# Where the maxima of staged weights stand among the steps of a two-branch attention kernel

## The chip, the core and the metric

The kernel runs on one core of one Trainium2 chip. The metric is the device time of one execution in microseconds (us). TensorE (PE), VectorE (DVE), ScalarE (ACT), GpSimd (POOL) and the queue of SyncE (SP), which issues most transfers, each work through their own list of instructions in order, and wait for one another by semaphores.

## What is computed

Two attention blocks over the same input, with 32 heads of 20 features each, mixed by a gate of one number per row:

```python
B, S, D = 1, 2048, 640; H = 32
qkv = (x @ wqkv).reshape(B, S, 3, H, 20)
p = softmax(einsum("bhqd,bhkd->bhqk", q, k) * 20 ** -0.5)
attend = einsum("bhqk,bhkd->bhqd", p, v).reshape(B, S, D) @ wo
g = sigmoid((A_x * gate_w).sum(-1, keepdims=True))
out = g * attend(A_x, A_wqkv, A_wo) + (1 - g) * attend(A_x, B_wqkv, B_wo)
```

## The kernel before

**Units and steps.** The 2 x 32 heads are cut into 16 groups of four heads (`g`, 0 to 15). For each group the 2048 queries are cut into four blocks of 512 (`qb`), and for each block the keys are worked through in eight steps (`NS`). That makes 512 steps, counted by `G`; group `g` begins at step `b = 32 g`. A step holds two **half-steps**. In each, PE makes four products of scores (L684, into a bank of PSUM), ACT takes their exponentials (L687, `pt`), and PE multiplies those by the values into the accumulator `acc` (L702, eight instructions). Beside that, PE makes scores of later units a first time (L626) so that DVE can take their row maxima (L637, or L630 on ACT with L634 on DVE), 15 steps ahead. There are seven banks that the products share; which one is taken is decided while the program is written, by a model of when each comes free (`take`, `give`, `spend`).

**Projections between.** A half-step may also hold a block of products of a projection (L419): queries and keys of a coming group (128, 168 or 176 columns wide), values (160), or outputs (up to 320). Weights are split in two 16-bit halves for this, after scaling by a power of two, so the largest absolute value of each weight matrix is needed first.

**The chain of a scale.** A piece of weights of 128 x 5 x 160 numbers is loaded into `wstage` (two buffers) by SP. DVE takes its largest absolute value (`largest`, L270). For the queries and keys, and for the output weights, `max_tasks` writes this in two pieces, rows 0:3 and rows 3:5 of the five, two turns apart. For the values, `weights_v` writes it in one. The maximum then goes through memory to all partitions: store (L212), ten turns, load into `srows` (L216), 18 turns, and then DVE's small instructions (L220 and `powers`), which give the factor (`r_v`, `r_qk`, `r_o`) that POOL splits the weights by. `scales_o` also makes the factors `f_o` of the output rows, by two DVE instructions on 128 x 16 numbers (L263, L265).

**What sets the order.** Nothing is scheduled by the chip. The step loop calls `scores` eight times in a step, in an order written out in `STEP`; after each, `advance()` lets every running side chain (`side`) go on to its next `yield`. One such turn is an eighth of a step. After the fourth, the tasks entered for that step by `at(G, ...)` are written. So `QKMAX`, `OMAX` and the numbers in the calls of `at` decide beside which step an instruction stands in each engine's list. `QKMAX` entries are loads and maxima in turn, two steps each; those of `OMAX` are load, factor (POOL, L280), maximum, one step each.

**Steps in which sums are turned.** After the second values of a step with `G % 8 == 0`, a block of queries is done. `take_acc` has DVE transpose `acc` into `ot` (L789), take a reciprocal (L794), and, six turns later, POOL scale it (L797); 16 turns after that, DVE transposes it again (L800). The next values (L702), half a step after the block's last, write `acc` anew and so have to wait for the first transpose. About one and a half steps after it stand the reduction and small transpose that end a block's maxima (L644, L647).

```python
if G % NS == 0 and k == 2 and G < STEPS:
    side.append(take_acc(*unit_of(G - 1)[:2]))
    advance()
```

Of the kernel before, what the change touches and what calls it, by code (L numbers as in the profile page):

```python
# [11 lines left out]
F32 = mybir.dt.float32  # L12
# [7 lines left out]
P = 128  # L20
# [22 lines left out]
OWAIT = 24  # L43
PACE = 2
AFROM, ADUE, ADUES = -24, -8, 4
QKMAX = (0, 10, 42, 10)
VEARLY = 338
OMAX, OSPLIT = (134, 346), (151, 362)
OUTS = ((166, 5.2), (257, 5.8), (398, 4.5), (466, 2.5))
OWAITS = (40, 20, 20, 10)  # L50
OFINE = (16, 16, 6, 16)
# [20 lines left out]
def kernel(  # L72
# [183 lines left out]
    def scales_v(gg, maxima):  # L256
        return scales_by_dram(maxima, 1, lambda r, inv: set_v(gg, r, inv))

    def scales_o(z, maxima):
        def then(r, inv):  # L260
            nc.vector.tensor_copy(r_o[z], r)
            yield
            nc.vector.tensor_scalar(f_o[z], gates[:, z, :], inv, inv_x, op0=OP.mult, op1=OP.mult)  # L263
            yield
            nc.vector.tensor_scalar(f_o[z], f_o[z], 1.0 / QKS, None, op0=OP.mult)  # L265

        return scales_by_dram(maxima, 1, then)

# [13 lines left out]
    def max_tasks(srcs, finish, by=None):  # L282


        m = wts.tile([P, 2, 8], F32, name="wmax", tag="wmax", bufs=2)
        tasks = []
        for k, parts in enumerate(srcs):
            for i, (src, c0) in enumerate(parts):
                st = {}

                def load(st=st, src=src, c0=c0):
                    st["t"] = weight_chunk(src, c0, 160)

                def factor(st=st):
                    by_rows(st["t"], by)

                def reduce(st=st, k=k, i=i):
                    largest(m[:, k, 2 * i:2 * i + 1], st["t"][:, 0:3])

                    def other():  # L300
                        yield
                        yield
                        largest(m[:, k, 2 * i + 1:2 * i + 2], st["t"][:, 3:NC])

                    side.append(other())

                tasks += [load, reduce] if by is None else [load, factor, reduce]

        def last():
            m2 = wts.tile([P, 2], F32, name="m2", tag="m2", bufs=2)  # L310
            n = len(srcs)
            nc.vector.tensor_reduce(m2[:, :n], m[:, :n, :2 * len(srcs[0])], axis=AX.X, op=OP.max)
            side.append(finish(m2))

        return tasks + [last]
# [236 lines left out]
    def weights_v(gg):  # L552

        z, i = divmod(gg, NG // 2)
        st = {}

        def load():
            st["t"] = weight_chunk(wqkv[z], 2 * D + i * 160, 160)

        def scale():  # L560
            m = wts.tile([P, 1], F32, name="m1", tag="m1", bufs=2)
            largest(m, st["t"])
            return scales_v(gg, m)

        def split():
            hi, lo = v_tiles(gg)
            split_weights(st["t"], r_v[gg], hi[:, :, :160], lo[:, :, :160])

        return load, scale, split
# [19 lines left out]
    def sigmoids():  # L589

        g, h = gates[:, 0, :], gates[:, 1, :]
        nc.vector.tensor_scalar(h, g, 1.0, None, op0=OP.add)
        nc.vector.reciprocal(g, h)
        nc.vector.tensor_scalar(h, g, -1.0, 1.0, op0=OP.mult, op1=OP.add)


# [483 lines left out]
        for k, f in enumerate(fs):  # L1080
            at(G + k * gap, f)

    at(4, sigmoids)
    step = NQ * NS
    for g in range(2 * NG):
        b = g * step
        n = g + 1
        if n < 2 * NG:
            parts = APARTS.get(n, 3)
            fill += [((-8, 15)[g] if g < 2 else b + AFROM, b + ADUE + ADUES * ch if g else 4 + 3 * ch, parts, project_a(n, ch))  # L1090
                     for ch in range(4)]
            if n + 1 < 2 * NG:
                tasks(b + 2 if g else 9, 3, weights_a(n + 1))
            i = g // 4 + 1
            if i < 4:
                if g % 4 == 0:
                    z, c0 = i // 2, 320 * (i % 2)
                    srcs = max_tasks([[(wqkv[z], part * D + c0 + 160 * k) for k in range(2)] for part in range(2)],
                                     lambda m, i=i: scales_qk(i, m))
                    tasks(b + QKMAX[i], 2, srcs)  # L1100
                if g % 4 == 2:
                    tasks(b + 6, 3, weights_r(i))
                    parts = RPARTS.get(i, 3)
                    fill += [(b + 12, b + 26 + 6 * ch if i == 1 else b + 22 + 4 * ch, parts, project_r(i, ch)) for ch in range(4)]
            gg = g // 2 + 1
            if gg < NG and g % 2 == 0:
                load, scale, split = weights_v(gg)
                at(max(b - 11, 0), load)
                if gg < NG - 1:
                    at(max(b - 8, 3), lambda scale=scale: side.append(scale()))  # L1110
                at(max(b - 1, 10), split)
                fill += [(max(b + 2, 12), b + 2 * step - 4 + j // 2, 2, project_v(gg, j)) for j in range(0, NT, 2)]
    early = weights_v(NG - 1)
# [165 lines left out]
```

## Time and profile before

| what | value |
|---|---|
| time, median of 3 runs (lowest to highest) | 2754.22 us (2753.87 to 2754.22) |
| the profiled execution's own time, its span | 2753.79 us, 2752.0 us |
| PE, DVE, ACT, POOL busy, share of the span | 99%, 89%, 92%, 24% |
| the chain that ended last | PE 93%, DVE 3%, ACT 1% |
| granted TensorE clock, mean | 0.997 |

A matmul's end is modelled in the profile, so a PE that stands still for a few tenths of a microsecond still shows as busy. A better measure of a half-step is the time from the start of one group of values (L702) to the start of the next.

### The profile page before, as it was taken

Reading aid. Unit: us, or ns where it says so; the run is one execution under the profiler, and the core shown is the slowest. Engines: PE = TensorE matmul, PEld = TensorE weight load, DVE = VectorE, ACT = ScalarE, POOL = GpSimd, SP = SyncE. Lnnn points to the kernel's source line nnn. Section 1 sums busy time; section 2 is a strip of 40 time slices with the busy share of each in tenths; the row PEclk is TensorE's granted clock in tenths of the full one; section 3 lists DMA queues with packets and bytes.
Section 4 is the critical chain, followed back from the end, with each engine's and each line's share of the span. In section 5 each row is a group of like instructions: output and inputs, shape, how many; then the busy total and the mean of one; then the engine's idle time right before and its main releaser. Section 6 shows DMA issues by size and latency. Waiting matters only on the chain.

```text
span 2752.0 us, 62213 instructions
## 1 busy us (share of the span) xinstructions
PE 2718.3 (99%) x23277; PEld 938.3 (34%) x23277; DVE 2441.0 (89%) x4785; ACT 2527.8 (92%) x5128; POOL 667.6 (24%) x909
## 2 busy tenths in 40 slices
PE   7999999999999999999999999999999999999999
PEld 3433333333333332333333333333333333333222
DVE  7789899999999989888888998989988898999992
ACT  4999999999999999999999999999999999999997
POOL 6232122222123421312221121222342202210111
PEclk8999999999999999999999999999999999999999
DMA  4021102010120211102012231221201112122112
GB/s 142 17 57 26 31 15 44 7 30 17 25 55 18 63 41 49 43 9 61 20 41 67 61 81 29 55 57 51 66 16 42 27 53 64 32 77 61 49 48 77
DMA packets 177008, 125.58 MB, mean 46 GB/s; under 512 B 105280, under 2 KB 147064, under 8 KB 176704
## 3 DMA queue, kind: packets, MB, share of 16 engines
q1 hardware_dynamic: 174160, 120.31, 17.2%
q8 instruction: 182, 2.98, 0.5%
q0 software_dynamic: 1600, 0.96, 0.2%
q14 instruction: 122, 1.00, 0.1%
q10 hardware_dynamic: 944, 0.33, 0.0%
HBM read 55.53 MB, written 31.86 MB: 32 GB/s over the span
## 4 chain that ended last, share of the span: by engine, by line
PE 93%; DVE 3%; ACT 1%; DMA 1%; POOL 1%; issue 0%; SPq 0%; POOLq 0%; ACTq 0%; DVEq 0%
PE acc L702 35%; PE bank L626 20%; PE bank L419 20%; PE bank L684 18%; DVE mpart L637 1%; ACT pt L687 1%; DMA ws<-in_A_wqkv_dram 0%; PE bank L878 0%; DVE rl L634 0%; DVE ot L789 0%; DMA kt<-mrow 0%; DMA xs<-in_A_x_dram 0%; DVE m L270 0%; ACT rl L630 0%; SPq L465 0%
## 5 line engine op out<-in xcount | busy, mean ns | idle before, releaser
L687 ACT ACTIVATE pt<-bank 128x512 f32<-128x512 f32 x4096 | 2166.3, 613 | 140.2 <-PE bank L684 97.5
L637 DVE TENSOR_REDUCE mpart<-bank 128x1 f32<-128x512 f32 x2944 | 1845.0, 681 | 219.4 <-PE bank L626 118.3
L702 PE MATMUL acc<-pt,v 128*21 128x512 f32 x8192 | 1081.7, 600 | 0.6 <-DVE ot L789 0.5
L684 PE MATMUL bank<-qt,kt 64*128 64x512 f16 x4096 | 1036.7, 380 | 1.7 <-DVE mpart L637 0.6
L626 PE MATMUL bank<-kt,qt 60*128 60x512 f16 x3520 | 1006.5, 380 | 4.5 <-ACT pt L687 2.2
L626 PEld LDWEIGHTS <-qt 60*128 60x128 f16 x4096 | 239.2, 94 | 900.6 <-issue 832.8
L634 DVE CUSTOM_DVE_ANT_0 rl<-bank,rl 128x512 f32<-128x512 f32 x576 | 386.5, 677 | 6.7 <-ACT rl L630 2.5
L630 ACT ACTIVATE rl<-bank 128x512 f32<-128x512 f32 x576 | 338.2, 597 | 7.3 <-PE bank L626 6.9
L684 PEld LDWEIGHTS <-kt 64*128 64x128 f16 x4096 | 230.2, 94 | 175.9 <-issue 65.4
L702 PEld LDWEIGHTS acc<-pt,v 128*21 128x21 f32 x8192 | 143.0, 99 | 428.7 <-issue 423.5
L419 PE MATMUL bank<-xx,wbh 128*128 128x168 f16 (+3 forms) x2480 | 287.7, 236 | 1.4 <-DVE wbh L958 1.0
L419 PE MATMUL bank<-xx,wbl 128*128 128x168 f16 (+3 forms) x1240 | 257.5, 235 | 0.0
L797 POOL TENSOR_TENSOR ot<-ot,sq 128x512 f32<-128x512 f32 x63 | 66.1, 1049 | 774.9 <-DVE sq L794 756.4
L419 PEld LDWEIGHTS <-wbh 128*128 128x128 f16 x2480 | 192.8, 98 | 111.1 <-issue 104.7
L626 PE MATMUL bank<-kd,qt 60*128 60x512 f16 x576 | 203.5, 379 | 0.7
L419 PE MATMUL bank<-woh,o_in 128*128 128x320 f16 (+3 forms) x700 | 157.7, 290 | 0.6 <-ACT pt L687 0.6
L419 PE MATMUL bank<-wvh,xx 128*128 128x160 f16 (+1 forms) x1280 | 156.7, 234 | 0.6 <-DVE mpart L634 0.6
L448 POOL CAST cq<-fs 128x512 f16<-128x512 f32 x60 | 36.7, 612 | 487.0 <-ACT fs L446 470.4
L419 PEld LDWEIGHTS <-xx 128*128 128x128 f16 x1920 | 131.1, 97 | 59.4 <-issue 56.5
L419 PE MATMUL bank<-wvl,xx 128*128 128x160 f16 (+1 forms) x640 | 137.7, 232 | 0.0
L419 PEld LDWEIGHTS <-wbl 128*128 128x128 f16 x1240 | 121.2, 98 | 4.3 <-issue 0.9
L419 PEld LDWEIGHTS <-o_in 128*128 128x128 f16 (+1 forms) x1050 | 87.4, 97 | 91.5 <-issue 68.2
(147 smaller groups left out, 1246.4 us busy)
## 6 DMA issues: line engine op xcount, KB each, us to landing
y_scr<-y_out SPq DMA_DIRECT2D x48, 320.0 KB
y_out<-y_scr SPq DMA_DIRECT2D x32, 320.0 KB
kt<-cq SPq DMA_DIRECT2D x120, 80.0 KB
o_scr<-on SPq DMA_DIRECT2D x240, 40.0 KB
o_in<-o_scr SPq DMA_DIRECT2D x64, 96.0 KB
kt<-cq SPq DMA_DIRECT2D x136, 40.0 KB
wstage<-in_B_wqkv_dram SPq DMA_DIRECT2D x13, 400.0 KB
xs<-in_A_x_dram SPq DMA_DIRECT2D x8, 640.0 KB
```

Source lines behind the costliest of these rows:

```text
L419: nc.tensor.matmul(out_ap, a, b, start=(k == 0), stop=(k == len(pairs) - 1))
L448: nc.gpsimd.tensor_copy(hi, f)
L626: nc.tensor.matmul(pt, QT[g % 2][r, pair, q0:q0 + P], k, start=True, stop=True)
L630: nc.scalar.activation(relus[u, j], pt, AF.Relu)
L634: nc.vector.tensor_tensor_reduce(rl, pt, rl, 1.0, LOW, OP.add, OP.max, m)
L637: nc.vector.tensor_reduce(m, pt, axis=AX.X, op=OP.max)
L684: nc.tensor.matmul(et, KT[g % 2][r, pair, kt * P:(kt + 1) * P], QT[g % 2][r, pair, qb * QB:(qb + 1) * QB], start=True, stop=True)
L687: nc.scalar.activation(pt, et, AF.Exp, scale=factor(g // 4))
L702: nc.tensor.matmul(acc[32 * h:32 * h + VW, :], V[(g // 2) % 2][:, kt, (g % 2) * GH + h, :], ptiles.pop((G, kk, h)), start=(kt == 0), stop= ...
L797: nc.gpsimd.tensor_tensor(t3, t3, sq.unsqueeze(2).to_broadcast([P, 16, 32]), op=OP.mult)
```

## The change

The first half of each staged maximum and its second half now stand six turns apart instead of two (`max_tasks`), and the values' maximum, which was one instruction, is made the same way with one small instruction that joins the halves. The steps at which they begin are moved: `QKMAX` from 10, 42, 10 to 11, 40, 11, `OMAX[0]` from 134 to 132, and the values' load and maximum one step later. `f_o` is made by one DVE instruction on one number per partition, and one POOL instruction on 128 x 16. The three small instructions that turn the gate's exponentials into the two gates are set two turns apart.

```diff
-QKMAX = (0, 10, 42, 10)
+QKMAX = (0, 11, 40, 11)
-OMAX, OSPLIT = (134, 346), (151, 362)
+OMAX, OSPLIT = (132, 346), (151, 362)
...
-            nc.vector.tensor_scalar(f_o[z], gates[:, z, :], inv, inv_x, op0=OP.mult, op1=OP.mult)
+            f = wts.tile([P, 1], F32, name="fo", tag="fo", bufs=1)
+            nc.vector.tensor_scalar(f, inv, inv_x, 1.0 / QKS, op0=OP.mult, op1=OP.mult)
             yield
-            nc.vector.tensor_scalar(f_o[z], f_o[z], 1.0 / QKS, None, op0=OP.mult)
+            nc.gpsimd.tensor_scalar(f_o[z], gates[:, z, :], f, None, op0=OP.mult)
...
                     def other():
-                        yield
-                        yield
+                        yield from turns(6)
                         largest(m[:, k, 2 * i + 1:2 * i + 2], st["t"][:, 3:NC])
...
         def scale():
-            m = wts.tile([P, 1], F32, name="m1", tag="m1", bufs=2)
-            largest(m, st["t"])
-            return scales_v(gg, m)
+            m = wts.tile([P, 3], F32, name="m1", tag="m1", bufs=2)
+            largest(m[:, 0:1], st["t"][:, 0:3])
+            yield from turns(6)
+            largest(m[:, 1:2], st["t"][:, 3:NC])
+            yield
+            nc.vector.tensor_reduce(m[:, 2:3], m[:, 0:2], axis=AX.X, op=OP.max)
+            yield from scales_v(gg, m[:, 2:3])
...
         nc.vector.tensor_scalar(h, g, 1.0, None, op0=OP.add)
+        yield from turns(2)
         nc.vector.reciprocal(g, h)
+        yield from turns(2)
         nc.vector.tensor_scalar(h, g, -1.0, 1.0, op0=OP.mult, op1=OP.add)
...
-    at(4, sigmoids)
+    at(4, lambda: side.append(sigmoids()))
...
-                at(max(b - 11, 0), load)
+                at(max(b - 10, 0), load)
                 if gg < NG - 1:
-                    at(max(b - 8, 3), lambda scale=scale: side.append(scale()))
+                    at(max(b - 7, 3), lambda scale=scale: side.append(scale()))
```

The lists of PE and ACT keep every instruction in its place; only the banks that they name differ from step 3 on. On DVE, one place is step 56, the turn of sums before the third group's values are needed. The list of before has there (`m` is the values' maximum, `rl,mpart` and `mpart` are row maxima of scores, `ot` and `sq` belong to the turn, `mneg` and `mt` to the end of a block's maxima):

```order
L270 TENSOR_REDUCE m_5311<-wstage 128x1
L634 ISA rl,mpart<-bank_94,rl 128x512
L634 ISA mpart 128x1
L789 STREAM_TRANSPOSE ot<-acc 128x512
L794 RECIPROCAL sq<-ot 128x16
L637 TENSOR_REDUCE mpart<-bank_91 128x1
```

The changed list, from behind the turn on, has:

```order
L271 TENSOR_REDUCE m_5388<-wstage 128x1
L643 TENSOR_REDUCE mpart<-bank_93 128x1
L643 TENSOR_REDUCE mpart<-bank_91 128x1
L650 TENSOR_REDUCE mneg_75<-mpart 128x16
L653 STREAM_TRANSPOSE mt<-mneg_75 128x32
L643 TENSOR_REDUCE mpart<-bank_90 128x1
L643 TENSOR_REDUCE mpart<-bank_89 128x1
L643 TENSOR_REDUCE mpart<-bank_91 128x1
L643 TENSOR_REDUCE mpart<-bank_92 128x1
L271 TENSOR_REDUCE m_5388<-wstage 128x1
L566 TENSOR_REDUCE m_5388<-m_5388 128x1
```

The maximum has gone from ahead of the transpose to one and two steps behind it, on either side of `mneg` and `mt`. The other place on DVE is the output factor of the first branch, in step 150 before (`es` is the maximum spread over the partitions and its powers, `r_o` and `f_o` what comes of it):

```order
L174 TENSOR_SCALAR es<-es 128x1
L261 COPY r_o_117<-es 128x1
L637 TENSOR_REDUCE mpart<-bank_91 128x1
L263 TENSOR_SCALAR f_o_119<-gates,es,inv_x 128x16
L637 TENSOR_REDUCE mpart<-bank_95 128x1
L265 TENSOR_SCALAR f_o_119<-f_o_119 128x16
```

After the change, about two steps sooner, DVE has:

```order
L174 TENSOR_SCALAR es<-es 128x1
L643 TENSOR_REDUCE mpart<-bank_92 128x1
L261 COPY r_o_117<-es 128x1
L264 TENSOR_SCALAR fo<-es,inv_x 128x1
L643 TENSOR_REDUCE mpart<-bank_94 128x1
```

and the product with the gates stands in POOL's list, behind the split of a turned block (`on`) and ahead of a projection's (`cq`):

```order
L809 CAST on<-ob 128x512
L810 TENSOR_TENSOR on<-ob,on 128x512
L266 TENSOR_SCALAR f_o_119<-gates,fo 128x16
L448 CAST cq<-fs 128x512
```

Two wide DVE instructions have become one narrow one, and POOL has one more.

## The prediction

> **What bounds the kernel now.** I read the page first, then the waits of PE, then the lengths of single half-steps.
>
> ```profile
> span 2752.0 us, 62213 instructions
> PE 2718.3 (99%) x23277; PEld 938.3 (34%) x23277; DVE 2441.0 (89%) x4785; ACT 2527.8 (92%) x5128; POOL 667.6 (24%) x909
> ```
>
> PE is the bound, and the change takes no work from it. So the only time to be won is time in which PE stands still for another engine. The waits of PE seem to leave almost none:
>
> ```profile
> PE bank L183 <- DVE wm L924: 11.0, 1, 11.0
> ...
> PE bank L626 <- ACT pt L687: 2.2, 8, 0.5
> ...
> PE bank L419 <- ACT pt L687: 0.6, 1, 0.6
> ```
>
> (engine, line, what it waited for: us in total, times, longest.) The largest is in the start, which the change leaves alone. But a modelled end hides short waits, so I compare half-steps, from one group of values to the next, with others that hold the same products. The first column is the stretch, the second its length; the rest is busy time and the number of instructions of each engine.
>
> ```profile
> core 0: us, PE busy (x) PEld busy (x) DVE busy (x) ACT busy (x) POOL busy (x), PEclk, DMA share, GB/s
> 350.28:353.55 3.27, 3.27 (x35) 1.37 (x34) 3.16 (x8) 3.27 (x8) 1.45 (x3) 1.00 0.00 0
> 187.51:191.37 3.86, 3.76 (x36) 1.47 (x34) 3.83 (x10) 3.86 (x10) 0.83 (x1) 1.00 0.03 6
> 228.02:231.93 3.91, 3.64 (x36) 1.39 (x34) 3.88 (x9) 3.87 (x9) 1.28 (x2) 1.00 0.02 4
> 390.95:394.71 3.76, 3.64 (x35) 1.40 (x34) 3.73 (x8) 3.71 (x9) 0.82 (x1) 1.00 0.02 0
> 793.16:797.07 3.91, 3.64 (x35) 1.39 (x33) 3.88 (x9) 3.87 (x9) 0.92 (x1) 1.00 0.18 41
> 1335.36:1338.98 3.62, 3.62 (x35) 1.49 (x33) 3.51 (x8) 3.56 (x9) 1.10 (x2) 1.00 0.01 2
> 1377.18:1380.96 3.78, 3.62 (x35) 1.58 (x33) 3.75 (x8) 3.66 (x9) 0.84 (x1) 1.00 0.02 0
> 1714.26:1718.03 3.77, 3.61 (x35) 1.57 (x33) 3.74 (x8) 3.65 (x9) 0.84 (x1) 1.00 0.02 0
> 1630.13:1633.74 3.61, 3.61 (x36) 1.56 (x34) 3.58 (x9) 3.41 (x8) 1.10 (x2) 1.00 0.55 108
> 996.84:1000.65 3.81, 3.81 (x35) 1.65 (x33) 3.78 (x9) 3.61 (x9) 0.82 (x1) 1.00 0.00 0
> 755.34:757.08 1.74, 1.74 (x17) 0.37 (x15) 1.74 (x4) 1.50 (x4) 1.66 (x3) 1.00 0.00 0
> 1551.20:1553.26 2.06, 2.06 (x17) 0.36 (x15) 2.06 (x5) 1.24 (x4) 0.00 (x0) 1.00 0.35 127
> 842.34:844.49 2.15, 2.11 (x17) 0.41 (x15) 2.08 (x6) 1.97 (x5) 0.83 (x3) 1.00 0.01 4
> 867.65:870.21 2.56, 1.92 (x16) 0.44 (x14) 2.56 (x5) 2.29 (x5) 1.48 (x2) 1.00 0.00 0
> 429.28:432.17 2.89, 2.71 (x19) 0.64 (x18) 2.85 (x8) 2.89 (x8) 0.55 (x1) 1.00 0.00 0
> 432.17:434.23 2.06, 2.06 (x16) 0.44 (x16) 2.06 (x4) 1.73 (x5) 0.55 (x2) 1.00 0.03 8
> 1038.47:1041.95 3.48, 2.77 (x19) 0.63 (x18) 3.45 (x8) 3.48 (x9) 0.00 (x0) 1.00 0.00 0
> 1041.95:1044.84 2.89, 2.39 (x16) 0.45 (x16) 2.89 (x7) 1.83 (x5) 1.10 (x2) 1.00 0.03 0
> 1584.55:1587.76 3.21, 3.21 (x26) 1.06 (x25) 3.13 (x9) 3.02 (x7) 0.00 (x0) 1.00 0.00 0
> 1579.02:1582.84 3.82, 3.57 (x30) 0.96 (x31) 3.75 (x14) 3.69 (x9) 0.00 (x0) 1.00 0.00 0
> ```
>
> The first row is a turn of sums with no maximum of weights beside it, with a projection 128 wide; the next four are such turns with one. They take 0.49 to 0.64 us longer, and DVE works through all of them but 0.03 us. What happens is seen on DVE's timeline of the first row and of the fourth (start, duration):
>
> ```profile
> 351.40 0.72 DVE L789 STREAM_TRANSPOSE ot<-acc 128x512 f32<-128x512 f32 x1
> ```
>
> ```profile
> 391.31 0.97 DVE L270 TENSOR_REDUCE m<-wstage 128x1 f32<-128x800 f32 x1
> ...
> 392.81 0.71 DVE L789 STREAM_TRANSPOSE ot<-acc 128x512 f32<-128x512 f32 x1
> ```
>
> The transpose begins 1.12 us after the stretch without a maximum (351.40 - 350.28), and 1.86 us with one (392.81 - 390.95). The next values must wait for it, and the banks wait for DVE's row maxima behind it. In a turn DVE is what ends PE's wait.
>
> **The change, part by part.** Durations are of the profiled execution, 2753.79 us, which lies 0.43 us below the median of the runs.
>
> *Maxima that leave turns of sums.* Ten turns lose theirs. Those 128 wide: 3.86, 3.91, 3.76 and 3.91 against 3.27: 0.59 + 0.64 + 0.49 + 0.64 = 2.36 us. Of three that are 160 wide the first and last are shown (1377, 1714): 3.78 and 3.77 against 3.62, so 0.16 each, 0.47 in all. The one 176 wide at 996 against 1630: 0.20, and I take as much for one at 1504. At 1551 a half-step without a projection follows its turn and takes 2.06 against 1.74: 0.32. Sum 3.55 us. The end below is about half of it, as the instructions still have to be done somewhere nearby.
>
> *The turn at 1038.* Here a piece of the queries' and keys' maxima and the values' maximum fall into one turn, in which PE also catches up on row maxima. The same kind of turn at 429 has neither: 3.48 against 2.89, then 2.89 against 2.06, and then PE waits 0.59 us for ACT's exponentials in the next half-step (the third wait above). Sum 0.59 + 0.83 + 0.59 = 2.0 us. After the change a single small instruction stands in that turn.
>
> *Output factors.* The half-step at 867 takes 2.56 against 1.74 us: 0.82 for these two instructions,
>
> ```profile
> L263 DVE TENSOR_SCALAR f_o<-gates,es,inv_x x2: 286/494/703, 867.3 to 1978.6; 128x16 f32<-128x16 f32 x2
> L265 DVE TENSOR_SCALAR f_o<-f_o x2: 164/446/728, 868.5 to 1979.4; 128x16 f32<-128x16 f32 x2
> ```
>
> (min/median/max in ns), which took 703 and 728 ns there, beside 1.48 us of POOL work in the stretch, and 286 and 164 ns in the second branch. What is left on DVE is one number per partition. Its price lies between the 0.16 us of the shorter and the 0.73 us of the longer; I take 0.16, since the powers of two ahead of it are as narrow. Gain 0.66. POOL's new instruction is written in step 148, and the first output product, which needs it, comes at step 166 (`OUTS`).
> [...]
>
> *Chains that move.* The values' chain of small instructions (L220 and on) stands about two steps later, the others from two steps sooner to one later. At 1579, one of them (14 DVE instructions in the stretch) costs 3.82 against 3.21 us; it moves into the next step, where it may cost from nothing to the same 0.61. I take half as gain, 0.3. The others I count at nothing: they leave one full half-step and come into another.
> The later chain gives POOL its factor later. POOL's split of the third group's values ended, and PE's first product with them began, here:
>
> ```profile
> 417.27 1.67 POOL L351 TENSOR_TENSOR wvl<-wstage,wvh 128x800 f16<-128x800 f32 x1
> ```
>
> ```profile
> 436.03 0.24 PE L419 MATMUL bank<-wvh,xx 128*128 128x160 f16 x1
> ```
>
> That leaves 17.1 us, and the order moves the factor by 15 turns, not quite two steps, or about 10 us. On SP's list the chain's load (L216) now stands behind the eight small transfers that end a block's maxima; the longest wait there is 3.9 us:
>
> ```profile
> SPq L662 <- DMA m_scr<-m4r: 53.1, 56, 3.9
> ```
>
> It is waited for 18 turns after its place, over two steps, so DVE should not stand for it. Cost nothing; without that cover, DVE would hold all row maxima behind L220.
>
> *Where the maxima go.*
>
> ```profile
> L270 DVE TENSOR_REDUCE m<-wstage x7: 973/974/982, 119.4 to 1866.7; 128x1 f32<-128x800 f32 x7
> ```
>
> ```profile
> L637 DVE TENSOR_REDUCE mpart<-bank 128x1 f32<-128x512 f32 x2944 | 1845.0, 681 | 219.4 <-PE bank L626 118.3 <-PE bank L684 94.9
> ```
>
> The seven whole maxima become 14 halves with seven joins. DVE idles 219.4 us ahead of its row maxima, 0.43 us for each of 512 steps, and the banks even out more than a step. Ten pairs now lie in the two steps behind a turn, next to the reduction and transpose that end a block's maxima. A pair of halves in one such step stands in the trace: 842, 2.15 against 1.74 us, so 0.41 is the upper price, and zero the lower (the half-step at 755 has none). As the halves are now a step apart, I take 0.06 each, 0.6 in all. Two second halves of output weights come into a turn; by the turns above, half of the 0.4 to 0.6 us for a pair: 0.2 each, 0.4. The first branch's output weights leave 842 and a like place: gain 0.2 net.
> [...]
>
> *Gates.* The three instructions are spread, but the first values' second half now falls beside them: nothing.
>
> Sum: 3.55 + 2.0 + 0.66 + 0.3 + 0.2 - 0.6 - 0.4 = 5.7 us. From 2753.79 that is 2748.1, and 0.43 us more as a median: 2748.5 us.
>
> **The rivals.**
>
> *Forecast, 0.53: PE gets the waits back and little comes in their place.* 2748.5 us. Its own range ends at 2748.7 above. Below, all gross gains without a new cost are 3.55 + 2.0 + 0.82 + 0.61 + 0.41 = 7.4 us, and the other banks may save as well as cost, say the 2.2 us of PE's waits for ACT in L626: 2754.2 - 7.4 - 2.2 = 2744.6.
>
> *The waits are given back in the new steps, 0.40.* DVE is 89% busy, and its work grows. Against it speaks the idle time of 0.43 us a step; for it, the pair at 842. If the ten pairs cost 0.41 each, 4.1 in place of 0.6, and the output factor's rest 0.73, the gain is 5.7 - 3.5 - 0.6 = 1.6: 2752.6 us. It decides from a price of 0.1 us a pair.
>
> *The banks fall out of step, 0.07, slower.* The model that picks banks is fed with other times, so from step 3 on PE names other banks. If it picks banks that ACT or DVE still hold, PE waits a little everywhere. To end over 0.2% above the median it must eat the 5.7 us and 5.5 more, 22 ns in each of 512 steps; at 35 ns it is 17.9 us, 2748.5 + 17.9 = 2766.4. Against it: before, PE waited for ACT in L626 only eight times, 2.2 us, and the values' maximum, counted as 0.5 us where it takes 0.97, is now counted as two halves.
>
> That the change doesn't do what it says is out: the order shows the maxima behind the turns.
>
> **How the numbers follow.** About 0.2%, 5.5 us, is what a measurement of this kernel can tell from no change. The forecast is just beyond it, so faster has 0.53, within 0.40, slower 0.07. The range reaches from the gross gains, 2744.6, to the second case without the chains' 0.3 as well, 2752.9, rounded up to 2753.0 for the runs' own spread.
>
> **What would show it.** Right: in the turn at about 390, the transpose begins some 1.1 us after the half-step's start, and the half-step takes 3.3 us; at 1038, 2.9 and 2.1; at 867, 1.75. Halves behind a turn leave their half-steps at the common length. Wrong: half-steps one and two steps behind turns grow by 0.2 us and more; L220 or a maximum waits for a transfer; PE's waits for banks appear where no maximum of weights is near.

## The result and the profile after

| kernel | median (lowest to highest) | ratio to before, 95% interval | profiled execution, its span |
|---|---|---|---|
| before | 2753.86 us (2753.09 to 2754.51) | | 2753.79 us, 2752.0 us |
| changed | 2749.65 us (2748.64 to 2750.14) | 0.9984, 0.9978 to 0.9990 | 2749.74 us, 2747.9 us |

The change saves 4.2 us, 0.15%, and the interval excludes no change. That is less than the 0.2%, about 5.5 us, that the prediction had set as its bound for "faster", so by its own bounds the result falls into the case to which it gave 0.40. 2748.5 us was forecast, with 2744.6 to 2753.0 as the range; the forecast's own case ended at 2748.7, and the median lies 0.95 us above that.

The head of the changed kernel's page:

```profile
span 2747.9 us, 62220 instructions
PE 2717.7 (99%) x23277; PEld 938.0 (34%) x23277; DVE 2441.2 (89%) x4797; ACT 2527.4 (92%) x5128; POOL 667.2 (24%) x911
```

No engine has less to do: DVE is as busy as before, in 12 instructions more. What is gone is time between instructions, and PE's line hides it, as it did before. The waits of PE (engine, line, what it waited for: us in total, times, longest), where L632 and L693 are the changed kernel's numbers for L626 and L687:

```profile
PE bank L183 <- DVE wm L930: 11.0, 1, 11.0
...
PE bank L632 <- ACT pt L693: 0.8, 4, 0.3
PE bank L690 <- ACT pt L693: 0.7, 2, 0.4
```

The 2.2 us that PE waited for ACT in the first products of scores are 0.8 now. The rest is seen by comparing half-steps. Windows of the changed kernel, on half-steps that the prediction showed for before (the stretch, its length, then busy time of each engine):

```profile
187.58:191.20 3.62, 3.62 (x36) 1.39 (x34) 3.39 (x9) 3.62 (x10) 1.10 (x2) 1.00 0.02 5
228.14:231.41 3.27, 3.27 (x35) 1.37 (x33) 3.16 (x8) 3.27 (x8) 1.42 (x3) 1.00 0.00 0
390.26:393.53 3.27, 3.27 (x35) 1.37 (x33) 3.16 (x8) 3.27 (x8) 1.06 (x2) 1.00 0.00 0
792.47:795.74 3.27, 3.27 (x35) 1.37 (x34) 3.16 (x8) 3.27 (x8) 1.06 (x2) 1.00 0.64 165
841.00:842.75 1.75, 1.75 (x16) 0.36 (x15) 1.75 (x4) 1.61 (x4) 0.83 (x3) 1.00 0.05 5
865.99:867.74 1.75, 1.75 (x17) 0.36 (x15) 1.75 (x4) 1.54 (x4) 1.53 (x2) 1.00 0.00 0
1035.77:1038.71 2.94, 2.71 (x19) 0.64 (x17) 2.90 (x9) 2.94 (x8) 0.53 (x1) 1.00 0.03 0
1038.71:1040.79 2.08, 2.08 (x16) 0.45 (x15) 2.08 (x4) 1.75 (x5) 0.57 (x2) 1.00 0.00 0
1546.85:1548.60 1.75, 1.75 (x17) 0.36 (x16) 1.75 (x4) 0.91 (x3) 0.00 (x0) 1.00 0.46 164
```

The turns at 228, 390 and 792, which took 3.91, 3.76 and 3.91 us, now take 3.27, the length of a turn without a maximum. The one at 187 stops at 3.62: ACT has ten instructions there, not eight, and is busy in all of it. The transposes of the sums begin 1.13 us after their half-steps' starts (391.39 - 390.26 and 793.60 - 792.47), as the timeline of DVE has it (start, duration):

```profile
391.39 0.72 DVE L795 STREAM_TRANSPOSE ot<-acc 128x512 f32<-128x512 f32 x1
```

```profile
793.60 0.72 DVE L795 STREAM_TRANSPOSE ot<-acc 128x512 f32<-128x512 f32 x1
```

The catch-up at 1038 went from 3.48 and 2.89 to 2.94 and 2.08, the output factors' half-step from 2.56 to 1.75.

Not all of that stays. The sum over the 1023 half-steps is -3.9 us, made of -12.2 in those that got shorter and +8.3 in those that got longer. These are some of the longer ones in the changed kernel:

```profile
145.00:149.52 4.52, 4.12 (x36) 1.62 (x34) 4.34 (x17) 4.28 (x10) 1.11 (x2) 1.00 0.24 48
395.28:398.64 3.36, 3.36 (x35) 1.39 (x33) 3.23 (x8) 3.36 (x8) 0.00 (x0) 1.00 0.03 7
418.71:421.60 2.89, 2.79 (x19) 0.56 (x18) 2.82 (x11) 2.89 (x8) 0.00 (x0) 1.00 0.74 160
421.60:424.11 2.51, 2.33 (x17) 0.45 (x16) 2.42 (x7) 2.18 (x6) 1.94 (x1) 1.00 0.30 70
1055.69:1058.15 2.46, 2.11 (x16) 0.44 (x15) 2.46 (x6) 2.29 (x5) 0.00 (x0) 1.00 0.08 7
1579.93:1583.76 3.83, 3.58 (x27) 0.97 (x25) 3.76 (x14) 3.70 (x8) 0.00 (x0) 1.00 0.00 0
```

And the same in the kernel before, except for the last, which the prediction showed (1584, 3.21):

```profile
145.78:149.40 3.62, 3.62 (x36) 1.60 (x34) 3.23 (x9) 3.62 (x9) 1.11 (x2) 1.00 0.28 57
396.49:399.72 3.23, 3.23 (x35) 1.40 (x33) 3.09 (x9) 3.21 (x8) 0.00 (x0) 1.00 0.12 8
420.37:422.87 2.50, 2.44 (x19) 0.64 (x18) 2.40 (x6) 2.50 (x7) 0.00 (x0) 1.00 0.15 33
422.87:424.83 1.96, 1.96 (x17) 0.54 (x16) 1.96 (x4) 1.96 (x6) 0.00 (x0) 1.00 0.00 0
1060.03:1061.77 1.74, 1.74 (x17) 0.44 (x15) 1.74 (x5) 1.57 (x4) 0.00 (x0) 1.00 0.71 181
```

The row at 395 holds a first half behind a turn. The other five hold a chain's small instructions (17 DVE instructions in place of 9 at 145, 14 in place of 9 at 1579), now in other half-steps than before; the one at 1055 holds only the start of a chain. Two of these chains came out of places that were as dear. At 410 and 413 the kernel before lost 0.94 us; the changed kernel saves that and loses it again at 418 and 421. The chain at 1579 cost as much in the half-step ahead of that one before the change (3.82 us, in the last of the prediction's windows).

### The profile page after: what moved, and what is told of

Its sections match the earlier page's. It is cut to its first block, busy times and chain, and to the rows that moved or that the text cites. A ratio compares the mean times of both kernels' runs of the same rounds, so it can differ in the third digit from the quotient of the medians.

```text
span 2747.9 us, 62220 instructions
## 1 busy us (share of the span) xinstructions
PE 2717.7 (99%) x23277; PEld 938.0 (34%) x23277; DVE 2441.2 (89%) x4797; ACT 2527.4 (92%) x5128; POOL 667.2 (24%) x911
## 3 DMA queue, kind: packets, MB, share of 16 engines
q1 hardware_dynamic: 174160, 120.31, 17.5%
## 4 chain that ended last, share of the span: by engine, by line
PE 96%; DVE 2%; ACT 1%; DMA 1%; issue 0%; POOL 0%; POOLq 0%; SPq 0%; DVEq 0%; ACTq 0%
PE acc L708 36%; PE bank L419 21%; PE bank L632 20%; PE bank L690 18%; ACT pt L693 1%; DVE mpart L643 1%; DMA ws<-in_A_wqkv_dram 0%; PE bank L884 0%; PE bank L938 0%; DMA xs<-in_A_x_dram 0%; DVE rl L640 0%; DVE ot L795 0%; ACT rl L636 0%; DVE wp L271 0%; POOL xx L888 0%
## 5 line engine op out<-in xcount | busy, mean ns | idle before, releaser
L693 ACT ACTIVATE pt<-bank 128x512 f32<-128x512 f32 x4096 | 2166.2, 613 | 137.7 <-PE bank L690 96.0
L632 PE MATMUL bank<-kt,qt 60*128 60x512 f16 x3520 | 1008.9, 381 | 2.4 <-ACT pt L693 0.8
L632 PEld LDWEIGHTS <-qt 60*128 60x128 f16 x4096 | 238.5, 94 | 896.6 <-issue 828.7
L632 PE MATMUL bank<-kd,qt 60*128 60x512 f16 x576 | 203.5, 379 | 0.7
```

The source lines that it names most:

```text
L632: nc.tensor.matmul(pt, QT[g % 2][r, pair, q0:q0 + P], k, start=True, stop=True)
L693: nc.scalar.activation(pt, et, AF.Exp, scale=factor(g // 4))
```

## The experiments

The theory to test: time goes by how much DVE work stands beside one half-step, each half-step hides a fixed piece, and a turn hides less. Rivals: the banks make the difference; or DVE, 89% busy, pays for work wherever it stands. The table has each run's medians, with the kernel before on the same chip, and the change of the sum over all half-steps in the profiled execution, which is free of what happens ahead of the first step and behind the last. The kernel before differs by up to 0.7 us from row to row, so a difference of less than 1 us between two rows is read from the half-steps.

| run | median, before beside it | ratio, 95% interval | half-steps, sum against before |
|---|---|---|---|
| changed | 2749.65, 2753.86 | 0.9984, 0.9978 to 0.9990 | -3.9 us |
| factors alone | 2752.19, 2753.23 | 0.9996, 0.9987 to 1.0005 | -1.0 |
| gates alone | 2752.78, 2753.23 | 0.9997, 0.9988 to 1.0006 | -0.5 |
| steps alone | 2750.46, 2753.23 | 0.9989, 0.9980 to 0.9998 | -3.4 |
| halves alone | 2754.47, 2753.23 | 1.0003, 0.9994 to 1.0013 | +0.4 |
| banks alone | 2752.87, 2753.51 | 0.9997, 0.9988 to 1.0006 | -0.5 |
| changed + work in turns | 2788.18, 2753.51 | 1.0126, 1.0110 to 1.0141 | +34.6 |
| changed + work between turns | 2774.96, 2753.51 | 1.0076, 1.0061 to 1.0092 | +21.1 |
| changed + the same, cut | 2756.63, 2753.84 | 1.0011, 1.0002 to 1.0021 | +3.6 |
| changed + cut, one in turns | 2775.05, 2753.84 | 1.0078, 1.0062 to 1.0093 | +21.4 |
| first chain out of the turn | 2748.77, 2753.51 | 0.9981, 0.9972 to 0.9990 | -4.6 |
| steps chosen again | 2747.66, 2753.84 | 0.9980, 0.9971 to 0.9989 | -5.5 |
| and chains spread | 2747.10, 2753.95 | 0.9975, 0.9965 to 0.9985 | -6.8 |

**One part of the change at a time.** Four runs put one part each into the kernel before.

The output factors:

```diff
-            nc.vector.tensor_scalar(f_o[z], gates[:, z, :], inv, inv_x, op0=OP.mult, op1=OP.mult)
+            f = wts.tile([P, 1], F32, name="fo", tag="fo", bufs=1)
+            nc.vector.tensor_scalar(f, inv, inv_x, 1.0 / QKS, op0=OP.mult, op1=OP.mult)
             yield
-            nc.vector.tensor_scalar(f_o[z], f_o[z], 1.0 / QKS, None, op0=OP.mult)
+            nc.gpsimd.tensor_scalar(f_o[z], gates[:, z, :], f, None, op0=OP.mult)
```

> The kernel before with the output factors alone made the new way. If PE's waits are local, made where DVE has too much in its list, the half-step at 867 us falls from 2.56 to 1.75 us and no other half-step moves by over 0.1 us: 0.8 us faster, 2753.1 from 2753.9. If the gain of the whole change comes from how the banks fall, nothing changes here, since the model that picks banks is fed with the same numbers: 2753.9. If VectorE's new small instruction is held up as the wide ones were, 0.1 to 0.3 us faster.

The half-step at 867 went from 2.56 to 1.74 us, all of its 0.82, and no other moved by 0.3. By the medians alone this can't be told from no change.

The gates:

```diff
         nc.vector.tensor_scalar(h, g, 1.0, None, op0=OP.add)
+        yield from turns(2)
         nc.vector.reciprocal(g, h)
+        yield from turns(2)
...
-    at(4, sigmoids)
+    at(4, lambda: side.append(sigmoids()))
```

> The kernel before with the gates' three instructions alone spread over turns. By the theory of local waits the half-step at 124.3 us falls from 4.01 to about 3.5 us and nothing else moves: 0.5 us faster, 2753.4. By the prediction's own term, nothing: 2753.9.

The half-step at 124 went from 4.01 to 3.48 us, and no other moved by 0.2. Windows of before and of this kernel:

```profile
124.29:128.30 4.01, 3.85 (x35) 1.52 (x33) 2.84 (x9) 3.56 (x8) 0.27 (x1) 1.00 0.04 2
```

```profile
124.05:127.53 3.48, 3.48 (x35) 1.52 (x34) 2.65 (x9) 3.47 (x8) 0.28 (x1) 1.00 0.06 2
```

PE's busy time falls short of the stretch by 0.16 us before, and not after. DVE is busy for only 2.84 of the 4.01 us, so here it is not the amount of its work that costs. Before, PE waits for a row maximum that stands behind the gates' three instructions:

```profile
126.05 0.37 PE L626 MATMUL bank<-kt,qt 60*128 60x512 f16 x1 [0.17 <-DVE mpart L634]
```

That is not the whole 0.53 us, and the banks have a part in it: the banks' run below moves no instruction, and takes this half-step to 3.69 us. In the changed kernel the first values' second half and its join, 0.63 us, stand where the three stood, and the half-step takes 3.49.

The moved steps, with the maxima as before (a whole one for the values, halves two turns apart for the others):

```diff
-QKMAX = (0, 10, 42, 10)
+QKMAX = (0, 11, 40, 11)
...
-OMAX, OSPLIT = (134, 346), (151, 362)
+OMAX, OSPLIT = (132, 346), (151, 362)
...
-                at(max(b - 11, 0), load)
+                at(max(b - 10, 0), load)
...
-                    at(max(b - 8, 3), lambda scale=scale: side.append(scale()))
+                    at(max(b - 7, 3), lambda scale=scale: side.append(scale()))
```

> The kernel before with the maxima moved to the new steps but not cut: the values' maximum is one instruction, the other halves stand two turns apart. If leaving the turns is what pays, the turns give back their 3.2 us and the turn at 1038 its 1.7 us; each whole pair right behind a turn costs about 0.4 us as the one at 842 did, ten of them 2 to 4 us if all do: 1 to 3 us faster, 2751 to 2753. If cutting in halves is what pays, no gain or a loss: 2754 to 2757.

The cut into halves six turns apart, at the steps of before:

```diff
-                        yield
-                        yield
+                        yield from turns(6)
                         largest(m[:, k, 2 * i + 1:2 * i + 2], st["t"][:, 3:NC])
...
-            m = wts.tile([P, 1], F32, name="m1", tag="m1", bufs=2)
-            largest(m, st["t"])
-            return scales_v(gg, m)
+            m = wts.tile([P, 3], F32, name="m1", tag="m1", bufs=2)
+            largest(m[:, 0:1], st["t"][:, 0:3])
+            yield from turns(6)
+            largest(m[:, 1:2], st["t"][:, 3:NC])
+            yield
+            nc.vector.tensor_reduce(m[:, 2:3], m[:, 0:2], axis=AX.X, op=OP.max)
+            yield from scales_v(gg, m[:, 2:3])
```

> The kernel before with the maxima cut and six turns apart, but begun in the old steps, so that one half stands in the turn and the other half a step behind it. If a turn of sums costs by the DVE time that stands ahead of its transpose, the turns lose about a third of their extra 0.16 to 0.64 us, 1 to 1.5 us in all, and the gain is 0 to 1.5 us: 2752.4 to 2753.9. If cutting alone is what pays, it gains as much as the whole change, 4.2 us: 2749.7.

Moving the steps brings most: 2.8 us of the 4.2, and 3.4 of 3.9 by half-steps. It also brings the whole 0.82 us at 867 without a new output factor, because `OMAX` takes that chain out of the half-step: in the changed kernel the two edits earn the same time, and it is earned once. What the moved whole maxima cost is seen in the windows of that kernel, one step behind the turn at 390 and two behind the one at 228:

```profile
395.60:399.29 3.69, 3.59 (x35) 1.30 (x33) 3.56 (x8) 3.64 (x9) 0.00 (x0) 1.00 0.04 5
236.50:238.73 2.23, 2.12 (x18) 0.35 (x16) 2.09 (x6) 2.05 (x5) 0.83 (x3) 1.00 0.00 0
```

That is 0.46 us over the 3.23 of before at the first, where the changed kernel, which has a half there, pays 0.13 (3.36). The second took 1.75 us in the kernel before, and takes that in the changed kernel, too. Cutting alone does nothing for the time; neither the 0 to 1.5 us nor the 4.2 us came. The turns get shorter, and the half-step behind them pays with the second half:

```profile
227.40:230.82 3.42, 3.42 (x35) 1.39 (x33) 3.38 (x8) 3.38 (x8) 1.20 (x2) 1.00 0.00 0
230.82:233.28 2.46, 2.11 (x15) 0.35 (x14) 2.46 (x6) 2.06 (x5) 0.28 (x2) 1.00 0.03 7
```

(windows of the kernel with the cut alone: 3.42 for 3.91, and then 2.46 for 1.74.) Nor does the cut add to the moved steps. The changed kernel is 0.5 us ahead of the run with the steps alone by half-steps, and the gates' half-step at 124 alone is 0.52 of that. The other half-steps win 6.1 us and lose 6.2: halves are cheaper behind turns than whole maxima (1.75 us for 2.23 at 236), but six turns between them also put the chains off, into dearer places such as 145, 741 and 1741. So the moved steps and the gates make the whole gain.

**The banks.** One line tells the model of work that doesn't exist:

```diff
     at(4, sigmoids)
+    at(3, lambda: spend("dve", 0.5))
```

> The kernel before, with one difference: at step 3 the model that picks the banks is told of 0.5 us of DVE work that does not exist. No instruction is added, left out or put elsewhere; PE and ACT only name other banks from step 3 on, as they do in the changed kernel. If the forecast's view holds (time goes by which DVE work stands beside which half-step, and the banks' numbers do not matter): within 0.5 us of before, no half-step moves by over 0.1 us. If the banks fall out of step (the rival): PE waits for ACT in L626 well over the 2.2 us of before, many half-steps grow by 0.02 to 0.04 us, and the time rises by 5 us or more.

No change that can be measured, and PE's wait for ACT in L626 stays at 2.2 us:

```profile
PE bank L626 <- ACT pt L687: 2.2, 8, 0.5
```

The expectation was not met to the letter: four half-steps moved by 0.2 to 0.3 us (124, 400, 1044, 1820), three of them down. So this other choice of banks shifts tenths in a few places, and nothing of the size that the rival needs. It is one choice of many.

**How much a half-step hides.** The changed kernel gets 57 extra maxima, whose result nothing uses, one in each of 57 turns, ahead of the transpose:

```diff
+    dm = consts.tile([P, 1], F32, name="dm")
+
+    def extra():
+        nc.vector.tensor_reduce(dm, ident.unsqueeze(1).to_broadcast([P, 6, P]), axis=AX.XY, op=OP.max, apply_absolute_value=True)
+
+    for G in range(24 + 0, 480, 8):
+        at(G, extra)
```

> The changed kernel, with an extra largest absolute value of 128 x 768 constant numbers on DVE, whose result nothing uses, in 57 steps with a turn of sums (G = 24, 32 and so on to 472), written behind the fourth scores of the step. It is about as long as a values' maximum before, 0.9 us. Theory of the turn (in a turn DVE ends PE's wait, so what stands ahead of the transpose is paid by PE): 0.2 to 0.6 us in each, by the 0.16 to 0.64 us that the ten maxima cost before, 57 x 0.3 = 17 us, 10 to 30. Rival (DVE is 89% busy and pays for work wherever it stands): the same as the next run, which has as many of them three steps from any turn.

Then the same with `range(24 + 5, 480, 8)`:

> The changed kernel, with the same 57 extra maxima of 128 x 768 numbers, but five steps behind each turn (G = 29, 37 and so on to 477), three ahead of the next. Theory of the turn: DVE has some 0.4 us idle a step, and the banks even out the rest over the next steps, so each costs 0 to 0.1 us, 0 to 6 us in all. Rival (work is paid wherever it stands): 57 x 0.3 us and more, as in the run with the extra maxima in the turns.

Both theories missed. The extra work is not free between turns (25.3 us over the changed kernel's median, where 0 to 6 were expected), and not as dear as in a turn (38.5). The half-steps say it more sharply. Groups of DVE by line (minimum, median, maximum in ns), in the first kernel and then a turn of it; and a half-step of the second kernel:

```profile
L1123 DVE TENSOR_REDUCE dm<-ident x57: 941/943/950, 227.7 to 2578.8; 128x1 f32<-128x768 f32 x57
```

```profile
227.37:231.31 3.94, 3.57 (x35) 1.37 (x33) 3.91 (x9) 3.65 (x9) 1.40 (x3) 1.00 0.00 0
```

```profile
252.38:256.03 3.65, 3.28 (x35) 1.38 (x33) 3.41 (x7) 3.36 (x8) 0.00 (x0) 1.00 0.26 52
```

The turn pays 0.67 us (3.94 for 3.27), and most turns pay 0.66 to 0.73, whatever projection stands beside them. The half-step between turns, which takes 3.23 us in the changed kernel, pays 0.42, and most of the others do. The steps behind pay next to nothing in both (2.3 us in all behind the turns, under 0.2 behind the others). In most of the turns, what is paid is what the transpose is late. In this one it begins 1.82 us after the start, 0.70 later than in the changed kernel:

```profile
229.19 0.71 DVE L795 STREAM_TRANSPOSE ot<-acc 128x512 f32<-128x512 f32 x1
```

So of 0.943 us a turn hides about 0.25 and another full half-step about 0.52, and what is over is paid at once; nothing is evened out later. If that is a price per instruction and not a proportion, cut work must cost less:

```diff
...
+        nc.vector.tensor_reduce(dm, ident.unsqueeze(1).to_broadcast([P, 3, P]), axis=AX.XY, op=OP.max, apply_absolute_value=True)
+
+    for G in range(24, 480, 8):
+        at(G + 5, extra)
+        at(G + 6, extra)
```

> The changed kernel, with the same extra work as in the run three steps ahead of the turns, cut in two: a maximum of 128 x 384 numbers at G = 29, 37 and so on, and another a step later, 114 in all. One of 128 x 768 took 0.943 us there and cost its half-step 0.42 us nearly everywhere, so some 0.52 us of it were hidden. Theory of the cover (each half-step hides about 0.52 us of DVE work, and only the rest is paid): a half takes about 0.54 us, costs 0.02 to 0.05, 1 to 6 us in all, against the 25 us of the uncut. Rival (all DVE work is paid at one rate, 0.44 of 0.94): 114 x 0.54 x 0.47 = 29 us, more than uncut.

And with `at(G, extra)` and `at(G + 1, extra)`:

> The changed kernel, with the same cut in two: a maximum of 128 x 384 numbers in each of the 57 turns of sums, and another one step behind. By the run with 0.943 us in the turns, a turn hides about 0.25 us. Theory of the cover: the half in the turn costs 0.54 - 0.25 = 0.29, the one behind it 0.02 to 0.1 (the end of a block's maxima stands there too): 17.5 to 22 us, against 38.5 us of the uncut. Rival (a turn pays in the same proportion whatever the length, 0.68 of 0.94): 57 x 0.54 x 0.72 = 22 us and the step behind as much as elsewhere, 57 x 0.25 = 14: 36 us.

Between turns the time over the changed kernel falls from 25.3 to 7.0 us, though DVE has more to do: 114 times 0.542 us are 61.8 us, and 57 times 0.943 are 53.8.

```profile
L1123 DVE TENSOR_REDUCE dm<-ident x114: 537/542/544, 252.6 to 2578.5; 128x1 f32<-128x384 f32 x114
```

```profile
252.23:255.48 3.25, 3.25 (x36) 1.40 (x34) 3.01 (x7) 3.25 (x8) 0.00 (x0) 1.00 0.25 56
```

The half-step that paid 0.42 pays 0.02, which is what 0.542 - 0.52 gives, and so do most of them. The 7.0 us lie a little above what was expected, because some ten half-steps, most beside other small work, still pay 0.2 to 0.5. With one half in the turns, most turns pay 0.27 to 0.30 (0.542 - 0.25 = 0.29):

```profile
227.01:230.55 3.54, 3.54 (x35) 1.32 (x33) 3.50 (x9) 3.54 (x9) 1.40 (x3) 1.00 0.00 0
```

That run took 25.4 us more than the changed kernel, between 17.5 to 22 for the cover and 36 for the proportion: 14.4 in the turns' half-steps, near the cover's 57 x 0.29 = 16.5 and not the proportion's 22, but 7.7 in the step behind them, between the cover's 1 to 6 and the proportion's 14. The end of a block's maxima and, every so often, halves already stand there.

**Better steps.** The first values' chain had slipped into the turn at 145, so its maximum begins one step sooner:

```diff
-                    at(max(b - 7, 3), lambda scale=scale: side.append(scale()))
+                    at(max(b - 7, 2), lambda scale=scale: side.append(scale()))
```

> The changed kernel, with the maximum of the first staged values begun one step sooner (step 2 in place of 3). In the changed kernel the six turns between its halves and the join push the chain's small instructions (L220 and on) into the turn of sums at step 8, whose half-step at 145 us grew by 0.90 us. If that is the cause, the half-step goes back to about 3.6 us, and the time falls by 0.9 us against the changed kernel, some 0.2 of it perhaps given back in step 7: 2748.8 us where that one has 2749.6. If the 0.90 us came from the banks or from a late transfer, it stays, and the time with it.

The turn is back at 3.62 us, 0.23 are given back in step 7; the half-steps fall by 0.7 us in all. Then all steps were chosen anew:

```diff
-QKMAX = (0, 11, 40, 11)
+QKMAX = (0, 11, 39, 8)
...
-OMAX, OSPLIT = (132, 346), (151, 362)
+OMAX, OSPLIT = (129, 346), (151, 362)
...
-                at(max(b - 10, 0), load)
+                e = 0 if b == 6 * step else 4
+                at(max(b - 10 - e, 0), load)
...
-                    at(max(b - 7, 3), lambda scale=scale: side.append(scale()))
+                    at(max(b - 7 - e, 2), lambda scale=scale: side.append(scale()))
```

> The changed kernel, with its steps chosen again by the cover of each half-step, so that neither a half nor a chain (L220 and on) stands in a turn of sums or in a half-step without a projection: QKMAX (0, 11, 39, 8) in place of (0, 11, 40, 11), OMAX[0] 129 in place of 132, the values' maximum four steps sooner for the groups 2, 3, 5 and 6, and the first one step sooner. By the half-steps of the changed kernel that stand above their like: step 8 0.9 us, steps 57 to 63 1.4, 126 0.3, 137 to 148 0.4, 188 0.7, 254 and 318 0.4, 274 to 287 1.2, in all 5.3 us. If two thirds of it come out, 3.5 us less than the changed kernel: 2746.1 us where that has 2749.6. Rival (the chain's small instructions are paid wherever they stand): only step 8 and the catching up at 62, 2.2 us at most, and 1 us given back in the steps 57 and 58, 121, 249, 313: 2748.4 us.

2747.66 us, 2.0 below the changed kernel's median: nearer to the rival than to the forecast; the half-steps fall by 1.6 us. Steps 8, 62, 63, 126, 144, 281, 282, 287 and 288 lose what they had too much, and the chains pay again where they now stand, 0.72 us more at 187, 0.65 at 284, 0.16 to 0.34 at 58, 122, 145, 250 and 314. The last run spreads the chain itself:

```diff
-        yield from powers(e.bitcast(I32), n)
-        yield from then(e[:, 3 * n:4 * n], e[:, 4 * n:5 * n])
+        for _ in powers(e.bitcast(I32), n):
+            yield from turns(gap)
+        for _ in then(e[:, 3 * n:4 * n], e[:, 4 * n:5 * n]):
+            yield from turns(gap)
...
-VEARLY = 338
+VEARLY = 335
```

> The kernel with its steps chosen again (steps of the changed kernel moved clear of turns and of half-steps without a projection), and the small DVE instructions of a chain (L220 and on) set four turns apart instead of one (two for the third maxima of queries and keys and the output weights, one for the fifth values), the last values' maximum three steps sooner for that. In the kernel it is built on, chains cost 0.72 us at step 187, 0.65 at 284, 0.55 at 58, 0.2 to 0.35 each at 7, 122, 145, 250 and 314, about 3.2 us in all. Theory of the cover (a half-step hides up to some 0.5 us of DVE work): one small instruction of 0.15 us in a half-step costs nothing, 0.1 at most in a turn, so 2.5 to 3 us less than that kernel: 2745 us where it has 2747.7. Rival (chains are paid wherever they stand, by their sum): 2747.7 us, no change.

Where the values' chains stood, the price is gone. Windows of the kernel with the steps chosen again, and of the spread one, of the same two half-steps:

```profile
398.91:402.69 3.78, 3.62 (x35) 1.31 (x34) 3.70 (x13) 3.74 (x9) 0.76 (x2) 1.00 0.06 8
718.37:722.15 3.78, 3.78 (x36) 1.49 (x34) 3.70 (x13) 3.65 (x9) 0.00 (x0) 1.00 0.07 7
```

```profile
398.39:401.70 3.31, 3.31 (x35) 1.31 (x33) 3.06 (x9) 3.27 (x8) 0.30 (x1) 1.00 0.06 6
717.61:721.05 3.44, 3.44 (x35) 1.49 (x34) 3.06 (x9) 3.32 (x8) 0.00 (x0) 1.00 0.06 7
```

9 DVE instructions stand where 13 did, and 3.78 us became 3.31 and 3.44. But 0.72 and 0.65 us at steps 187 and 284 stay: there one reduction of 128 x 256 numbers at a chain's head (L220), which this run leaves whole, stands among row maxima. The half-step of step 188 shows the same in the changed kernel: with that reduction it takes 2.46 us (1055 above), where the kernel before, with one of 128 x 128, took 1.74 (1060 above). These are the two in the changed kernel:

```profile
L220 DVE TENSOR_REDUCE es<-srows 128x2 f32<-128x256 f32 x3 | 1.2, 414 | 0.0
L220 DVE TENSOR_REDUCE es<-srows 128x1 f32<-128x128 f32 x9 | 2.4, 272 | 0.0
```

So a half-step without a projection hides less, and there the price jumps: 0.14 us more on DVE cost 0.72. The second half in the run with the cut alone (0.47 us, 2.46 for 1.74 at 230) paid as much. On the whole the half-steps fall by 1.2 us where 2.5 to 3 were expected, and the medians by 0.6. Against before, this kernel is the fastest that ran: 2747.1 us, 0.9975 (0.9965 to 0.9985). That it beats the changed kernel is seen in the half-steps (-6.8 against -3.9 us); the intervals of the two ratios overlap.

## Why the prediction came out as it did

The direction was right, and so was the mechanism for the turns, the catch-up and the output factors; the saving was 4.2 us where 5.7 was forecast. Of the signs named, those at 390, 1038 and 867 came out. Halves behind turns did not leave their half-steps at the common length: these grew by 0.1 to 0.34 us, two of them by more than the 0.2 us that the prediction had named as a sign of being wrong. The total is as near as it is partly by luck: two terms gained more than was foreseen (gates 0.5, output weights 0.9), and without them the half-steps would have fallen by 2.5 us and not 3.9. Term by term:

- **Turns that lose a maximum.** 3.55 us foreseen, 3.2 measured over the same ten half-steps. Nearly all that is missing is the turn at 187: 0.59 was booked, by comparing it with a turn that has eight ACT instructions and not ten, and 0.24 came. The transpose begins 1.13 us after the start, where 1.1 was named.
- **The turn at 1038.** 2.0 foreseen, 1.7 measured: 0.54, 0.81 and 0.31 us in three half-steps.
- **Output factors.** 0.66 foreseen. Measured 0.82 at 867, less 0.12 where the chain now stands, 0.70 in all. The new narrow instruction took 0.20 us, near the lower bound:

```profile
L264 DVE TENSOR_SCALAR fo<-es,inv_x x2: 200/202/204, 854.9 to 1974.6; 128x1 f32<-128x1 f32 x2
855.20 0.33 POOL L266 TENSOR_SCALAR f_o<-gates,fo 128x16 f32<-128x16 f32 x1 [4.50 <-DVE fo L264]
```

The upper bound, 0.73 us, did not come. In the changed kernel POOL had stood idle for 4.50 us until this instruction was done. In the run with the factors alone, it began 0.06 us ahead of a cast on POOL, and took 0.20 us all the same, where the wide one had begun as far ahead of the same cast and taken 0.70. The two of before, and the two of that run:

```profile
867.30 0.70 DVE L263 TENSOR_SCALAR f_o<-gates,es,inv_x 128x16 f32<-128x16 f32 x1
867.36 0.61 POOL L448 CAST cq<-fs 128x512 f16<-128x512 f32 x1 [14.93 <-ACT fs L446]
```

```profile
866.93 0.20 DVE L264 TENSOR_SCALAR fo<-es,inv_x 128x1 f32<-128x1 f32 x1
866.99 0.61 POOL L449 CAST cq<-fs 128x512 f16<-128x512 f32 x1 [14.92 <-ACT fs L447]
```

Why the wide ones took 0.70 and 0.73 us there, and 0.29 and 0.16 in the second branch, is not shown. What the prediction did not see is that moving `OMAX` earns this term by itself.

- **Gates.** Counted at nothing; 0.52 us gained. The step that failed is the belief that the first values' second half would take up what the spread sets free. It does stand there, and costs nothing. The half-step had been 4.01 us, with three instructions in a row, and its excess over the 3.48 us of steps like it could have been read from the trace.
- **Output weights.** 0.2 gain less 0.4 cost foreseen; 0.7 gained. Leaving 842 and 812 brought 0.41 and 0.28, the second half that came into the turn at 832 costs 0.18, as foreseen, and the second branch, whose cut second halves moved without `OMAX[1]`, gained 0.93 at 1902 and 1950 and gave 0.74 back at 1935 and 1951.
- **Halves behind turns.** 0.6 foreseen for ten pairs, 1.9 measured. This is the first term that was mis-sized. It was worked out from DVE's mean idle time, 0.43 us a step, and from the belief that banks even out more than a step. The runs with extra work show both wrong: 0.52 us are hidden in one half-step, and nothing later. First halves take longer than that:

```profile
L271 DVE TENSOR_REDUCE wmax<-wstage 128x1 f32<-128x480 f32 x20 | 12.9, 643 | 0.0
L271 DVE TENSOR_REDUCE wmax<-wstage 128x1 f32<-128x320 f32 x20 | 9.5, 476 | 0.0
```

0.643 - 0.52 = 0.12 us is what steps 17, 25, 57 and 137 pay (0.11, 0.13, 0.135 and 0.135). A second half of 0.476 us would be free by itself, and pays 0.1 to 0.3 where other small work stands beside it.

- **Chains.** 0.3 gain foreseen, about 1.3 lost. This is the other term that was mis-sized, and the larger one: 1.6 us. "I count the others at nothing: they leave one full half-step and come into another" fails, because half-steps are not equally full. The first chain came into a turn (0.90 us, gone in the run with that chain a step sooner), one came to 188, a half-step without a projection (0.72), and 0.62 at 1579 moved to the next step in full, where half of it was booked as gain.

The rival of waits given back held in part: 8.3 us came back in new places, more than the prediction's costs of 1.0 us, but more than half of it from chains (some 4.5 us), and 1.9 from the maxima on which the rival was built. The rival of the banks did not come about: one other choice of banks changed nothing that can be measured, and in the changed kernel, which has the banks in question, PE waited less for ACT in L632, not more. Cutting does make more work for DVE: 0.643 + 0.476 us for the two halves, 0.974 for the whole, 0.145 more a cut. It need not cost time, as the cut work shows: 8 us more of DVE work, 18 us less time.

What stays open: why a half-step hides 0.52 us and a turn 0.25. DVE's idle time in the changed kernel's half-step at 253 is 0.59 us (2.64 busy of 3.23) and in the turn at 390 0.11, so idle time alone does not give both numbers.

```profile
253.36:256.59 3.23, 3.23 (x36) 1.40 (x34) 2.64 (x6) 3.23 (x8) 0.00 (x0) 1.00 0.22 47
```

That a turn pays what its transpose is late holds for most turns with extra work (0.70 us late, 0.67 to 0.70 paid; with a half 0.30 late, 0.27 to 0.30 paid), but not for the kernel before: there the transpose in the turn at 390 was 0.73 us late, and the turn paid 0.49. Nor is the jump at 1055 and 230 traced to its first cause; the timeline shows only that PE then waits 0.35 us for ACT:

```profile
1057.85 0.37 PE L690 MATMUL bank<-qt,kt 64*128 64x512 f16 x1 [0.35 <-ACT pt L693]
```

## What to carry to other kernels

Price a small instruction by what its place still hides, not by the engine's mean idle time: add a known piece of work to many places at once, and read from start to start what each pays. Work that is over the cover is worth cutting and setting a step apart where both pieces find room, as the extra work did (7.0 us in place of 25.3). In the change itself the cut brought nothing, neither alone nor on top of the moved steps: second halves and the chains behind them came into other full places. When a chain is moved, look at the half-step in which every one of its instructions lands: here what two chains had paid in their old places, 0.94 us at 410 and 413 and 0.62 at 1579, came back in the new ones.

## What was not expected of the hardware

In the profiled executions of four of the fourteen kernels (the cut alone, the work between turns, the cut with one in turns, and the spread chains), the end behind the last full half-step took 15.8 to 16.1 us instead of 14.6. The granted clock fell there: it was 0.51 for 3.5 us in the spread kernel, and 0.57, 0.61 and 0.57 in stretches of 4 us at the ends of the other three. Windows of the spread kernel, and of the one with the steps chosen again, of the same stretch (the eighth column, behind POOL, is the granted clock):

```profile
2735.00:2738.50 3.50, 3.50 (x14) 1.83 (x15) 1.33 (x3) 1.26 (x5) 2.41 (x5) 0.51 0.13 47
```

```profile
2735.00:2738.50 3.50, 3.31 (x23) 2.24 (x23) 1.99 (x6) 1.57 (x7) 1.79 (x5) 1.00 0.00 0
```

14 products in place of 23 in the same 3.5 us, at 0.51 of the clock, with the mean over the span still 0.997 in both. It explains why these two kernels have the same span, 2745.6 us, though the half-steps differ by 1.2 us. Why some executions have it is not shown; a difference of 1 us between two single executions of this kernel is read from the half-steps, not from the spans.
